# One head and batch per partition for q, k and v, with kv on four row groups

## The chip, the cores and the metric

The kernel runs on one core of a Trainium2 chip. Its time is the device time of one execution in microseconds (us). Five engines work side by side: TensorE (PE, with its weight loads as PEld), VectorE (DVE), ScalarE (ACT), GpSimd (POOL) and SyncE (SP). Each takes its instructions in order and waits on semaphores for the others. Sixteen DMA engines move data between HBM and the on-chip memory (SBUF); here POOL, SP and ACT issue the transfers. PE writes its sums to PSUM.

## The reference

All data is float32. A linear attention is followed by a mixing of the sequence's 64 lowest frequencies.

```python
# q, k, v: (8, 8, 576, 64); w_phi: (64, 128)
def phi(x):
    proj = np.einsum('bhsd,df->bhsf', x, w_phi)
    proj = proj - np.max(np.abs(proj), axis=-1, keepdims=True)
    return np.concatenate([np.exp(proj), np.exp(-proj)], axis=-1)
q_p, k_p = phi(q), phi(k)
kv = np.einsum('bhsf,bhsd->bhfd', k_p, v)
z = np.sum(k_p, axis=2)
num = np.einsum('bhsf,bhfd->bhsd', q_p, kv)
den = np.einsum('bhsf,bhf->bhs', q_p, z)[..., None] + 1e-06
# x: num / den as (8, 576, 512); w_r, w_i: (64, 512, 512); w_ch: (512, 512)
X = np.fft.rfft(x, axis=1); Xr, Xi = X.real[:, :64], X.imag[:, :64]
Yr = einsum('bmd,mde->bme', Xr, w_r) - einsum('bmd,mde->bme', Xi, w_i)
Yi = einsum('bmd,mde->bme', Xr, w_i) + einsum('bmd,mde->bme', Xi, w_r)
u = x + irfft(Yr + 1j * Yi, n=576)      # the other frequencies are 0
out = u + maximum(u @ w_ch, 0)
```

The two weight arrays hold 134 MB, q, k and v together 28 MB, the output 9.4 MB.

## The kernel before

**Units.** The attention is cut into 16 units: a group g of two heads (four of them) by a pair bp of two batches (four). A unit has 4 x 576 = 2304 rows of 64 values of each of q, k and v. They lie in SBUF as 128 partitions x 18 rows. A partition belongs to a head (64 partitions each) and holds nine neighbouring rows of the first batch and nine of the second: `(h p) b (c d)`, with c = 9 in `load` (L94). Chunk n of 18 is column n of this layout. `load_k` and `load_q` convert to bf16 on the way; `load_v` (L121) keeps float32. POOL issues them, but SP the first two units' v; the last unit's v is issued by SP in three parts of 57, 64 and 7 partitions (`load_v_parts`, L113).

**A unit's steps.** `turn_k` and `turn_q` (L125) transpose two columns at a time on PE and ACT copies the result to kT and qT, which hold features on partitions. `rows` (L153) multiplies by w_phi (`w2blk` holds it twice, for two columns) with rows on partitions, and DVE takes the largest absolute value per row: mk for k, m for q. `exp_k` (L173) exponentiates k's product with both signs on ACT (AB). k's largest values go into v instead: `weigh_v` makes ee, `weigh_v2` multiplies v by it into va, and a 65th column makes z. `kv` (L201) contracts AB with va over the rows, 64 partitions of one head at a time, into two `one` buffers; ACT copies the sums to kvz (`keep_kv`). For q, `shift_q` (L223) turns m and makes mT, `cols_q` (L239) makes the product with features on partitions and subtracts the largest value by a second product, and `exp_q` (L260) exponentiates it with both signs (AQ). `num` (L276) contracts AQ with kvz, and DVE divides into xs. `freq` (L305) takes x to frequencies with the table CF, and `keep_x` keeps them in XT.

**The order.** Every engine's instructions stay in the order in which the program gives them (`InOrder`, L27; each of these instructions has L37 in the profile). The loop from L534 handles, in one pass, the steps of four neighbouring units: P (frequencies), Q (kv and num), K (rows and exponentials) and R (transposes). The part of a pass that the prediction speaks of, in order: `Q.exp_q(0)`, `K.rows_k(0)`, `K.exp_k(0)`, `Q.weigh_v2()` and the load of a later v, `P.freq()`, `P.keep_x()`, `Q.cols_q(1)`, `Q.exp_q(1)`, `K.rows_k(1)`, `K.exp_k(1)`, `Q.kv()`, `K.rows_q(0)`, `K.rows_k(2)`, `K.rows_q(2)`, `K.rows_q(1)`, `Q.cols_q(2)`, `Q.keep_kv()`, `Q.exp_q(2)`, `K.exp_k(2)`, `K.weigh_v()`, `R.turn_k`, `K.shift_q()`, `Q.num(0)`, `K.cols_q(0)`, `R.turn_q`, `Q.num(12)`.

**Buffers.** PSUM is given out by two helpers: `one` (L69), four buffers of one bank, and `two` (L72), two buffers of two banks, each taken in turn; a new use waits for the last reader of the buffer's old content. Inputs have two buffers each (`pin`).

**Weights.** 64 loads of w_r and w_i (tile wt: one real or imaginary array, eight modes, 128 of 512 channels; 2.1 MB read, stored as bf16) go through nine slots and a few borrowed places. `next_w` (L374) issues a load on POOL and `mix` (L480) uses it; `some` (L519) puts mixes into the passes. After the loop the rest of the weights are mixed (L1031 on), while `fill` runs the work of the output: `Channels` (x times w_ch), `Absorb` and the inverse tables. When the last weights have come, `finish` and `Pair` (L869) make the last sums and store the output by SP, two row chunks at a time; `back` (L767) picks the inverse table's column for a chunk.

Of the kernel before, what the change touches and what calls it, by code (L numbers as in the profile page):

```python
# [10 lines left out]
F32 = mybir.dt.float32  # L11
BF16 = mybir.dt.bfloat16
# [31 lines left out]
def kernel(  # L44
# [49 lines left out]
    def load(t, src, g, bp, eng):  # L94
        eng.dma_start(
            t.rearrange("p b c d -> p b (c d)"),
            src[2 * bp:2 * bp + 2, 2 * g:2 * g + 2].rearrange("b h (p c) d -> (h p) b (c d)", c=9),
        )


    class Unit:
# [3 lines left out]
        def load_k(self):  # L105
            self.kb = pin.tile([128, 2, 9, D_], BF16, name="kb")
            load(self.kb, k, self.g, self.bp, pool)

        def load_q(self):
            self.qb = pin.tile([128, 2, 9, D_], BF16, name="qb")  # L110
            load(self.qb, q, self.g, self.bp, pool)

        def load_v_parts(self):  # L113
            self.vn = pin.tile([128, 2, 9, D_], F32, name="vn")
            dst = self.vn.rearrange("p b c d -> p b (c d)")
            src = v[2 * self.bp:2 * self.bp + 2, 2 * self.g:2 * self.g + 2].rearrange(
                "b h (p c) d -> (h p) b (c d)", c=9)
            for p0, p1 in ((0, 57), (57, 121), (121, 128)):
                sp.dma_start(dst[p0:p1], src[p0:p1])

        def load_v(self, eng=pool):  # L121
            self.vn = pin.tile([128, 2, 9, D_], F32, name="vn")
            load(self.vn, v, self.g, self.bp, eng)

        def turn(self, src, dst, flat, part):  # L125

            rows = src.rearrange("p i c d -> p (i c d)")
            lo, hi = ((0, 4), (4, 9))[part]
            ptr = one([128, hi - lo, 128], BF16)
            for j in range(lo, hi):  # L130
                if flat or j < 4:
                    pe.transpose(ptr[:, j - lo, :], rows[:, j * 128:(j + 1) * 128], ident_b)
                elif j < 8:
                    n = 9 + 2 * (j - 4)
                    pe.transpose(ptr[:, j - lo, :], rows[:, n * 64:n * 64 + 128], ident_b)
                else:
                    for i in range(2):
                        pe.transpose(ptr[64 * i:64 * i + 64, j - lo, :], src[:, i, 8, :], ident_b)
            act.copy(dst[:, lo:hi, :], ptr)

# [49 lines left out]
        def weigh_v2(self):  # L190
            ee = self.ee
            self.va = pm.tile([128, 2, 18, 65], BF16, name="va", bufs=1)
            dve.tensor_copy(self.va[:, :, :, 64], ee)
            for ab in range(2):
                dve.tensor_tensor(
                    out=self.va[:, ab, :, 0:64], in0=self.vn.rearrange("p i c d -> p (i c) d"),
                    in1=ee[:, ab, :].unsqueeze(2).to_broadcast([128, 18, 64]), op=ALU.mult,
                )
            self.kvz = pm.tile([128, 2, 2, 2, 65], BF16, name="kvz", bufs=1)

        def kv(self):  # L201
            pk = [one([128, 2, 2, 65]) for h in range(2)]
            for i in range(2):
                for ab in range(2):
                    for c in range(9):
                        n = 9 * i + c
                        for h in range(2):
                            r = slice(64 * h, 64 * h + 64)
                            pe.matmul(
                                pk[h][:, i, ab, :], lhsT=self.AB[n // 8][r, ab, n % 8, :],  # L210
                                rhs=self.va[r, ab, n, :],
                                start=(i == ab == c == 0), stop=(i == ab == 1 and c == 8),
                            )
            self.pk2 = pk

        def keep_kv(self):
            for h in range(2):
                act.copy(self.kvz[:, h], self.pk2[h])

# [40 lines left out]
        def exp_q(self, i):  # L260
            if i == 0:
                self.AQ = []
            if i < 2:
                t = pm.tile([128, 2, 2, 2, 2, 64, 2], BF16, name="AQ", bufs=3)
            else:
                t = pm.tile([128, 2, 2, 128], BF16, name="AQr", bufs=1)
            for ab in range(2):
                if i < 2:
                    o = t[:, ab].rearrange("f c j h p a -> f a c (j h) p")
                    src = self.pa.rearrange("f c (a j) (h p) -> f a c (j h) p", a=2, h=2)  # L270
                else:
                    o, src = t[:, ab], self.pa
                act.activation(o, src, ACT.Exp, scale=1.0 - 2.0 * ab)
            self.AQ.append(t)

        def num(self, n0):  # L276

            pn = one([128, 6, 65])
            for n in range(n0, n0 + 6):
                h = n % 2  # L280
                if n < 16:
                    i, c = n // 8, n % 8 // 2
                    for ab in range(2):
                        pe.matmul(
                            pn[:, n - n0, :],
                            lhsT=self.AQ[i][:, ab, c % 2, c // 2, h].rearrange("f p a -> f (p a)"),
                            rhs=self.kvz[:, h, i, ab, :], start=(ab == 0), stop=(ab == 1),
                        )
                else:
                    for i in range(2):  # L290
                        r = slice(64 * i, 64 * i + 64)
                        for ab in range(2):
                            pe.matmul(
                                pn[r, n - n0, :],
                                lhsT=self.AQ[2][:, ab, i, 64 * h:64 * h + 64],
                                rhs=self.kvz[:, h, i, ab, :], start=(ab == 0), stop=(ab == 1),
                            )
# [7 lines left out]
        def freq(self):  # L305
            g, bp = self.g, self.bp
            px = one([128, 4, 2, 2, 32])
            for i in range(2):
                for out, d, t in ((px[:, 0:4:3, :, i], 0, slice(0, 2)),
                                  (px[:, 2, :, i], 1, 0), (px[:, 1, :, i], -1, 1)):  # L310
                    for c in range(5):
                        n = 8 * i + 2 * c if c < 4 else 16
                        at = 16 + ((g * NP + bp) * 18 + n) * D_ + d
# [78 lines left out]
    for p0 in (0, 64):  # L392
        pool.iota(si[p0:p0 + 64, 4:5], [[1, 1]], base=8, channel_multiplier=9)
    pi = const.tile([128, 1], I32, name="pi")
    pool.iota(pi, [[0, 1]], base=0, channel_multiplier=1)
    nine = const.tile([128, 64], F32, name="nine")
    pool.iota(nine.bitcast(I32), [[9, 64]], base=0, channel_multiplier=0)
    mi = scr[:, 2048:2112].bitcast(I32)
# [20 lines left out]
    dve.tensor_copy(odd[:, 0:1], odd[:, 2:3].bitcast(I32))  # L419
    dve.tensor_scalar_mul(out=odd[:, 1:2], in0=odd[:, 0:1], scalar1=-0.5)  # L420
    dve.tensor_scalar(out=sf[:, 0:4], in0=sf[:, 0:4], scalar1=0.5, scalar2=odd[:, 1:2],
# [112 lines left out]
    for n in range(-2, len(units) + 1):  # L534
# [55 lines left out]
        elif R and n + 4 == len(units):  # L590
            kept = pin.tile([128, 2, 9, D_], BF16, name="kb").rearrange(
                "p b c d -> p (b c d)")[:, 0:1024].rearrange("p (f m) -> p f m", m=8)
            assert not any(key[0] == 1 for key in mixq)
# [83 lines left out]
    def inverse_tables():  # L677
# [6 lines left out]
        for c in range(4):  # L684
            for a in range(2):
                dve.tensor_scalar_add(
                    out=tok[:, 128 * c:128 * c + 128].rearrange("k (p a) -> k a p", a=2)[:, a],
                    in0=nine, scalar1=float(4 * a + c))
        for i in range(2):
            dve.tensor_scalar_add(out=tok[:, 512 + 64 * i:576 + 64 * i], in0=nine, scalar1=8.0)  # L690
        used = [0, 0]
# [52 lines left out]
    class Channels:  # L744
# [15 lines left out]
        def product(self):  # L760
# [4 lines left out]
            act.copy(xw[:, self.bp, self.n, :], pf)  # L765

    def back(p, c, bp, table, src, r, start):  # L767

        if c < 8:
            pe.matmul(p, lhsT=table[r, c % 4, :], rhs=src[r, 2 * bp + c // 4, :],  # L770
                      start=start, stop=True)
# [97 lines left out]
    class Pair:  # L869
# [32 lines left out]
        def sums(self, side, a):  # L902
            (bp, n), at, z = self.items[a], self.at(side, a), self.z(side)
            start = not self.based(side)
            if self.straight:
                pe.matmul(at, lhsT=CM[n // 4][:, n % 4], rhs=ends[z], start=start,
                          stop=True)
# [28 lines left out]
        def store(self):  # L936
# [3 lines left out]
            for p in parts:  # L940
                a = slice(p[0], p[-1] + 1)
                self.add(a)
                if self.n8:
                    sp.dma_start(
                        bass.AP(tensor=out.tensor, offset=out.offset + (2 * bp * S_ + 8) * DMODEL,
                                ap=[[9 * DMODEL, 128], [2 * S_ * DMODEL, 2], [1, DMODEL]]),
                        self.o)
                else:
                    rows = out[2 * bp + n // 4]
                    sp.dma_start(  # L950
                        bass.AP(tensor=rows.tensor,
                                offset=rows.offset + (n % 4 + p[0]) * DMODEL,
                                ap=[[9 * DMODEL, 64], [4 * DMODEL, 2], [1, len(p) * DMODEL]]),
                        self.o[:, a].rearrange("p a e -> p (a e)"))
# [197 lines left out]
```

## Time and profile before

| what | us |
|---|---|
| three runs, median (lowest to highest) | 431.27 (430.65 to 433.17) |
| the profiled execution | 430.94 |
| its span, first to last instruction | 428.7 |
| PE busy, PEld busy | 321.2, 195.5 |
| DVE busy | 303.6 |
| ACT busy | 300.6 |
| POOL busy | 127.8 |
| end of the loop over units | 284 |
| last weights landed | 393 to 396 |

The mean granted TensorE clock was 0.94. Busy times add up over stages that differ: the loop over units, the rest of the weights with the output's work, and the tail. PE's busy time counts pipelined products. The page gives groups of instructions as `engine op out<-in, shape xcount | busy, mean ns | idle before`; a timeline line begins with the start and length in us and ends with the idle time before it and what ended it.

### The profile page before, as it was taken

The page shows a single profiled execution, that of the slowest core. Times are in us where ns is not written, and L with a number is a line of the kernel's source. Part 1 is how long each engine was busy: PE and PEld are TensorE (multiplying, and loading weights), DVE is VectorE, ACT ScalarE, POOL GpSimd, SP SyncE. Part 2 cuts the span into 40 slices and gives each one's busy share as a digit, 9 for nine tenths or more (in the row PEclk, how much of TensorE's full clock was granted, in tenths as well). Part 3 has the DMA queues.
Part 4 walks back from the last instruction along what each step waited for, and adds up shares of the span by engine and source line. Part 5 has one row for each costly group of instructions (what it writes and reads, how often), then busy time and mean ns, then how long its engine had stood idle before and what let it go on. Part 6 is the DMA issues. An engine that isn't in the chain of part 4 may idle for free.

```text
span 428.7 us, 10215 instructions
## 1 busy us (share of the span) xinstructions
PE 321.2 (75%) x4243; PEld 195.5 (46%) x4291; DVE 303.6 (71%) x592; ACT 300.6 (70%) x490; POOL 127.8 (30%) x167
## 2 busy tenths in 40 slices
PE   1666676678696677786795767867899789878994
PEld 1345555456364445554564545543454333333321
DVE  6668668766776776877877858868645546964695
ACT  3788788896887996977978848766644335553883
POOL 6232132123121213213122321220122037691661
PEclk9989799989999998998989969898999989999998
DMA  9999999999999999999999999999999999999798
GB/s 215 209 211 211 237 214 238 219 231 238 240 210 230 220 238 238 238 210 240 210 240 218 232 240 233 212 211 213 212 212 212 212 212 212 212 212 194 190 398 344
DMA packets 50040, 97.71 MB, mean 228 GB/s; under 512 B 2379, under 2 KB 11723, under 8 KB 49995
## 3 DMA queue, kind: packets, MB, share of 16 engines
q0 software_dynamic: 45152, 85.27, 101.6%
q1 hardware_dynamic: 4682, 11.73, 7.6%
q8 instruction: 33, 0.54, 0.5%
q10 hardware_dynamic: 160, 0.07, 0.1%
q14 instruction: 13, 0.10, 0.1%
HBM read 163.64 MB, written 9.44 MB: 404 GB/s over the span
## 4 chain that ended last, share of the span: by engine, by line
DMA 34%; PE 24%; ACT 22%; DVE 14%; issue 4%; POOL 1%; ACTq 0%; POOLq 0%; DVEq 0%
DMA wt<-in_moe_w_i_dram 28%; ACT AQ L37 9%; PE one L37 8%; PE pt L37 8%; DMA kb<-in_k_dram 6%; ACT AB L37 6%; DVE m L37 6%; PE two L37 5%; PE pp L37 3%; ACT qT L37 2%; ACT XT L37 2%; DVE xw L37 2%; DVE mk L37 1%; DVE mT L37 1%; DVE xs L37 1%
## 5 line engine op out<-in xcount | busy, mean ns | idle before, releaser
L37 ACT ACTIVATE AQ<-two 128x1024 bf16<-128x1024 f32 x64 | 80.5, 1347 | 2.2 <-PE two L37 2.1
L37 ACT ACTIVATE AB<-two 128x1024 bf16<-128x1024 f32 x64 | 62.7, 1051 | 4.5 <-DVE mk L37 4.2
L37 DVE TENSOR_REDUCE m<-two 128x8 f32<-128x1024 f32 x32 | 39.1, 1223 | 19.9 <-PE two L37 19.6
L37 POOL DMA_DIRECT2D wt<-in_moe_w_i_dram x30 | 22.2, 739 | 85.3 <-PE one L37 44.1
L37 DVE TENSOR_REDUCE mk<-two 128x8 f32<-128x1024 f32 x32 | 38.9, 1219 | 9.4 <-PE two L37 9.4
L37 ACT CAST xw<-pt 128x512 bf16<-128x512 f32 x39 | 22.9, 586 | 31.8 <-PE pt L37 31.6
L37 DVE TENSOR_TENSOR va<-vn,ee 128x1152 bf16<-128x1152 f32 x32 | 42.8, 1383 | 1.8 <-DMA vn<-in_v_dram 1.8
L37 PE MATMUL pt<-wchb,xT 128*128 128x512 bf16 x135 | 37.8, 394 | 7.2 <-DVE xT L37 2.4
L37 PE MATMUL two<-w2blk,qT 128*128 128x256 bf16 x128 | 21.9, 299 | 24.0 <-ACT AQ L37 12.3
L37 POOL DMA_DIRECT2D wt<-in_moe_w_r_dram x32 | 23.6, 739 | 52.6 <-PE one L37 25.9
L37 PEld LDWEIGHTS <-xs 128*128 128x128 bf16 x624 | 31.2, 102 | 13.3 <-issue 6.8
L37 ACT COPY qT<-one 128x512 bf16<-128x512 bf16 (+1 forms) x32 | 19.0, 642 | 20.8 <-PE one L37 20.7
L37 PEld LDWEIGHTS <-qT 128*128 128x128 bf16 x144 | 14.5, 103 | 38.2 <-issue 34.9
L37 PEld LDWEIGHTS <-XT 128*32 128x32 bf16 x584 | 16.8, 148 | 29.8 <-issue 16.9
L37 POOL DMA_DIRECT2D kb<-in_k_dram x16 | 11.4, 713 | 62.1 <-PE one L37 47.8
L37 PE MATMUL two<-mT,minus 96*128 96x512 bf16 x64 | 26.2, 410 | 2.9 <-issue 0.7
L37 DVE TENSOR_TENSOR xs<-one,rd 128x384 bf16<-128x384 f32 x48 | 26.8, 557 | 1.6
L37 PE MATMUL one<-wt,XT 128*32 128x512 bf16 x272 | 23.9, 439 | 3.4 <-ACT XT L37 3.4
L37 DVE TENSOR_TENSOR xs<-pa,xs 128x512 bf16<-128x512 f32 x27 | 17.7, 685 | 12.1 <-PE pa L37 10.3
L37 PE MATMUL one<-kvz,AQ 128*128 128x65 bf16 x512 | 25.3, 200 | 1.1 <-ACT qT L37 0.8
L37 PEld LDWEIGHTS <-AQ 128*128 128x128 bf16 x512 | 22.6, 103 | 7.0 <-issue 3.0
L37 POOL TENSOR_TENSOR xw<-rl,xw 128x512 bf16<-128x512 f32 x20 | 22.7, 1169 | 7.9 <-ACT rl L37 7.6
(161 smaller groups left out, 733.5 us busy)
## 6 DMA issues: line engine op xcount, KB each, us to landing
wt<-in_moe_w_r_dram POOLq DMA_DIRECT2D x29, 1024.0 KB, 27.7
wt<-in_moe_w_i_dram POOLq DMA_DIRECT2D x27, 1024.0 KB, 28.0
out_dram<-of SPq DMA_DIRECT2D x15, 512.0 KB, 3.6
vn<-in_v_dram POOLq DMA_DIRECT2D x13, 576.0 KB, 25.1
kb<-in_k_dram POOLq DMA_DIRECT2D x16, 288.0 KB, 21.4
qb<-in_q_dram POOLq DMA_DIRECT2D x16, 288.0 KB, 19.7
xs<-in_moe_w_i_dram POOLq DMA_DIRECT2D x2, 1024.0 KB, 23.9
out_dram<-of SPq DMA_DIRECT2D x6, 256.0 KB, 4.1
```

Of the source, the lines that this page charges most:

```text
L37: ins = f(*args, **kwargs)
```

## The change

A partition now holds 18 neighbouring rows of one head and one batch. For q and k the partition is (head, 32, batch) and a load is one transfer; v's partition is (batch, head, 32) and a load is two transfers of 64 partitions, one a batch. ACT's copies of the transposed q and k sort the batches apart, so that AB's partitions match va's. kv works on four groups of 32 partitions; its sums lie in one `two` buffer and two `one` buffers, and keep_kv takes three copies instead of two. The last v comes in four parts. AQ is written as one run with its input read across four columns. The row numbers behind the tables for the frequencies and the output's rows follow the new layout. The loop, the order of the steps and the weights' loads stay.

```diff
     def load(t, src, g, bp, eng):
         eng.dma_start(
-            t.rearrange("p b c d -> p b (c d)"),
-            src[2 * bp:2 * bp + 2, 2 * g:2 * g + 2].rearrange("b h (p c) d -> (h p) b (c d)", c=9),
+            t.rearrange("p c d -> p (c d)"),
+            src[2 * bp:2 * bp + 2, 2 * g:2 * g + 2].rearrange("b h (p c) d -> (h p) b (c d)", c=18),
         )
...
         def load_v_parts(self):
...
-            for p0, p1 in ((0, 57), (57, 121), (121, 128)):
-                sp.dma_start(dst[p0:p1], src[p0:p1])
+                "b h (p c) d -> b (h p) (c d)", c=18)
+            for p0, p1 in ((0, 57), (57, 64), (64, 121), (121, 128)):
+                sp.dma_start(dst[p0:p1], src[p0 // 64, p0 % 64:(p1 - 1) % 64 + 1])
 
         def load_v(self, eng=pool):
-            self.vn = pin.tile([128, 2, 9, D_], F32, name="vn")
-            load(self.vn, v, self.g, self.bp, eng)
+            self.vn = pin.tile([128, 18, D_], F32, name="vn")
+            dst = self.vn.rearrange("p c d -> p (c d)")
+            src = v[2 * self.bp:2 * self.bp + 2, 2 * self.g:2 * self.g + 2].rearrange(
+                "b h (p c) d -> b (h p) (c d)", c=18)
+            for b in range(2):
+                eng.dma_start(dst[64 * b:64 * b + 64], src[b])
...
             for j in range(lo, hi):
-                if flat or j < 4:
...
+                m = j if flat or j > 7 else 2 * (j % 4) + j // 4
+                pe.transpose(ptr[:, j - lo, :], rows[:, m * 128:(m + 1) * 128], ident_b)
+            act.copy(dst[:, lo:hi, :].rearrange("p j (b q) -> p j b q", b=2),
+                     ptr.rearrange("p j (q b) -> p j b q", b=2))
...
         def kv(self):
-            pk = [one([128, 2, 2, 65]) for h in range(2)]
-            for i in range(2):
+            low = two([128, 2, DMODEL])[:, :, 0:130].rearrange("p h (a d) -> p h a d", a=2)
+            high = [one([128, 2, 65]) for h in range(2)]
+            out = [low[:, 0], low[:, 1]] + high
+            for i in range(3):
                 for ab in range(2):
-                    for c in range(9):
-                        n = 9 * i + c
-                        for h in range(2):
-                            r = slice(64 * h, 64 * h + 64)
+                    for n in range(8 * i, min(8 * i + 8, 18)):
+                        for p in range(4):
+                            r = slice(32 * p, 32 * p + 32)
                             pe.matmul(
-                                pk[h][:, i, ab, :], lhsT=self.AB[n // 8][r, ab, n % 8, :],
+                                out[p][:, ab, :], lhsT=self.AB[i][r, ab, n % 8, :],
                                 rhs=self.va[r, ab, n, :],
...
         def keep_kv(self):
+            low, high = self.pk2
+            act.copy(self.kvz[:, :, 0], low)
             for h in range(2):
-                act.copy(self.kvz[:, h], self.pk2[h])
+                act.copy(self.kvz[:, h, 1], high[h])
...
             if i < 2:
-                t = pm.tile([128, 2, 2, 2, 2, 64, 2], BF16, name="AQ", bufs=3)
+                t = pm.tile([128, 2, 2, 2, 2, 32, 4], BF16, name="AQ", bufs=3)
...
                 if i < 2:
-                    o = t[:, ab].rearrange("f c j h p a -> f a c (j h) p")
-                    src = self.pa.rearrange("f c (a j) (h p) -> f a c (j h) p", a=2, h=2)
+                    o = t[:, ab].rearrange("f c b h p a -> f c (b h p) a")
+                    src = self.pa.rearrange("f c a s -> f c s a")
...
-    dve.tensor_scalar_mul(out=odd[:, 1:2], in0=odd[:, 0:1], scalar1=-0.5)
+    dve.tensor_scalar_mul(out=odd[:, 1:2], in0=odd[:, 0:1], scalar1=-8.0)
+    dve.tensor_tensor(out=sf[:, 4:5], in0=sf[:, 4:5], in1=odd[:, 1:2], op=ALU.add)
+    dve.tensor_scalar(out=odd[:, 2:3].bitcast(I32), in0=pi, scalar1=0, scalar2=3,
+                      op0=ALU.logical_shift_right, op1=ALU.bitwise_and)
+    dve.tensor_copy(odd[:, 1:2], odd[:, 2:3].bitcast(I32))
+    dve.tensor_scalar_mul(out=odd[:, 1:2], in0=odd[:, 1:2], scalar1=-0.5)
...
-        for i in range(2):
-            dve.tensor_scalar_add(out=tok[:, 512 + 64 * i:576 + 64 * i], in0=nine, scalar1=8.0)
+        for a in range(2):
+            for i in range(2):
+                at = 512 + 64 * i
+                dve.tensor_scalar_add(
+                    out=tok[:, at:at + 64].rearrange("k (p a) -> k a p", a=2)[:, a],
+                    in0=nine.rearrange("k (p a) -> k a p", a=2)[:, 0], scalar1=float(16 + a))
...
                 if self.n8:
+                    for i, (bp, n) in enumerate(self.items):
+                        sp.dma_start(
...
+                                    ap=[[18 * DMODEL, 64], [DMODEL, 2], [1, DMODEL]]),
+                            self.o[:, i])
+                else:
+                    b, j = place(n)
+                    rows = out[2 * bp + b]
                     sp.dma_start(
...
+                        bass.AP(tensor=rows.tensor, offset=rows.offset + (j + p[0]) * DMODEL,
+                                ap=[[18 * DMODEL, 32], [4 * DMODEL, 4], [1, len(p) * DMODEL]]),
```

## The prediction

> **What bounds the kernel now.** I read the page first, its slices and the line on HBM, to see which resource is never idle.
>
> ```profile
> span 428.7 us, 10215 instructions
> ...
> DMA  9999999999999999999999999999999999999798
> ...
> HBM read 163.64 MB, written 9.44 MB: 404 GB/s over the span
> ```
>
> The DMA engines are full in every slice until the last three. Reads are over at about 393 us (next view): 163.64 MB / 393 us = 416 GB/s. Then the chain of waits, in order of time, for what ends last.
>
> ```profile
> 328.49 37.24 DMA wt<-in_moe_w_i_dram
> 366.01 27.12 DMA wt<-in_moe_w_i_dram
> 393.18 0.67 PE pt L37 x12
> ```
>
> A weight load issued at 328.49 lands at 365.73, one issued at 366.01 at 393.13. By the timeline of POOL, four whole loads (2.10 MB read each) and four of 0.79 MB land between those two: 11.5 MB in 27.4 us, 421 GB/s. So the stream is a queue about 27 us deep that runs at one rate in bytes, and its last landing starts a tail of 35.6 us. Third, the waits of PE from 330 to 395 us (us in total, times, longest), to see how far compute is behind that stream.
>
> ```profile
> PE pt L37 <- DMA wt<-in_moe_w_i_dram: 3.1, 2, 1.6
> ...
> PE pt L37 <- DMA wt<-in_moe_w_r_dram: 1.5, 2, 1.2
> ```
>
> PE waits for weights 4.6 us in all, and from 284 to 330 us not once. Landings set beside the products that read them say the same: the products come 3 to 9 us after the landing until 330 us, 0.5 to 6 until 377, and within 0.1 us from 380 us on. Two bounds lie close together: the stream, and compute with some 4.5 us to spare. Fourth, the loop over units, which ends at 284 us: PE, then ACT, around one kv.
>
> ```profile
> 60.33 0.60 PE L37 MATMUL two<-w2blk,kT 128*128 128x256 bf16 x4 [0.75 <-ACT AB L37]
> 60.86 0.98 PE L37 MATMUL one<-va,AB 64*128 64x65 bf16 x50
> ...
> 63.42 0.60 PE L37 MATMUL two<-w2blk,qT 128*128 128x256 bf16 x4 [1.24 <-ACT AQ L37]
> ```
>
> ```profile
> 60.82 2.55 ACT L37 ACTIVATE AQ<-two 128x1024 bf16<-128x1024 f32 x2
> 63.14 2.02 ACT L37 ACTIVATE AB<-two 128x1024 bf16<-128x1024 f32 x2
> 64.93 0.77 ACT L37 CAST kvz<-one 128x260 bf16<-128x260 f32 x2
> ```
>
> kv's 72 products run from 60.86 to about 62.2, hidden under AQ. rows_q(0) starts at 63.42, the moment AQ ends, since it takes over the `two` buffer that AQ read. From there the chain goes on through two reductions (m), the shift (mT), cols_q(0), the copies qT, and AQ of the next unit: AQ ends again at 78.5, a period of 15.1 us.
>
> **The change, part by part.** Durations are of the profiled execution: 430.94 us, of which 428.7 are span; the runs have a median of 431.27, so one stands for the other.
>
> *The new wait.* kv's sums now lie in one `two` buffer and two `one` buffers. `two` has two buffers taken in turn; the order was rows_k(0), cols_q(1), rows_k(1), rows_q(0), rows_q(1), cols_q(0), and kv comes in fourth. So kv takes the buffer of cols_q(1) and waits for AQ (63.4); rows_q(0), which had that buffer, now takes that of rows_k(1) and waits for AB, two exponentials of 1.05 later: 65.5. rows_q(1) takes kv's buffer and waits for the copy kvz after it. kv itself is 144 products of 32 rows in place of 72 of 64. Now one takes 1.34 us / 72 = 19 ns with two row groups; four groups side by side give 10 ns (1.4 us), no gain from the smaller groups 19 ns (2.7 us). The first hides under AB. So rows_q(0) is late by 2.1 to 2.8 us; I take 2.4, between them. The trace has no product of 32 contracted rows beside three others. Queued behind kv on PE are rows_q, rows_k(2), cols_q(2) and the transposes of the next k, and DVE's reductions wait for those. In seven units PE already waits for kvz after kv (8.5 us in all); there 1.2 us of the delay is there today, and 0.65 to 1.4 is left; I take 1.0. Of the 15 passes with both kv and rows_q: 8 x 2.4 + 7 x 1.0 = 26.2 us (ends 21.4 and 32.2).
>
> [...]
>
> *q's exponentials.* AQ and AB do the same arithmetic on 1024 elements; AQ writes every other bf16, AB a run.
>
> ```profile
> L37 ACT ACTIVATE AQ<-two 128x1024 bf16<-128x1024 f32 x64 | 80.5, 1347 | 2.2 <-PE two L37 2.1
> L37 ACT ACTIVATE AB<-two 128x1024 bf16<-128x1024 f32 x64 | 62.7, 1051 | 4.5 <-DVE mk L37 4.2
> ```
>
> The new AQ writes runs but reads elements 512 B apart. Nothing in this trace reads so. Bounds: 1051 (as AB) and 1347 (the penalty only moves to the other side). I take 1051, because its writes are then AB's; 4 x 0.296 = 1.18 us a pass, all on the chain, 17.7 us over 15.
>
> *Copies and setup.* qT's and kT's copies read every other element: free, or slower in AQ's ratio (1.28), 0.33 us a pass for qT's 1.18 us on the chain, 5 in all; kT's are covered by mT and cols_q. I take 1. One transpose fewer a unit saves 0.06 us off the path. Four more small DVE operations of 0.15 to 0.25 us stand ahead of ident_b, for which PE waits 8.7 us at the start: 0.7 late. Two more operations of 0.28 us in the inverse tables, on the chain at 286: 0.5.
>
> *Compute in sum:* 26.2 - 17.7 + 1 + 0.7 + 0.5 = 10.7 us, less 4.5 to spare: +6.2. Ends: 21.4 + 1.2 - 17.7 - 4.5 = +0.4 and 32.2 + 6.2 - 17.7 - 4.5 = +16.2.
>
> *The stream.* k and q: 32 loads, each 256 packets of 1152 B written becoming 128 of 2304. By the packets' own lengths two of 107 ns become one of about 173 x 4608/4096 = 195: 19 ns x 4096 / 16 engines = 4.9 us, over the 1.12 by which packets overlap 4.3. By landings a k or q load comes 1.42 us after the one before it, and its bytes at a weight's rate (4.95 us for 2.10 MB) are 1.39: 32 x 0.03 = 1.0 us. The queue delivers by landings: -1.0. v has packets of 4608 B already (1.46 us a load) and its bytes stay; two halves at today's rate cost nothing. The last v, on SP: the 57-row part runs on three engines (its packets come by threes), 38 packets each of 2304 B. Two 57-row parts are 38 each of 4608 B: 38 x 88 ns = 3.3 us more on these, less 0.7 for the 64-row part. They ran 3 to 4 us ahead of the slowest, and now use that up; then all weights land that much later: +2 (ends 0 and +2.6). 2,300 more instructions add 7 fetch packets to 33 of 0.95 us: +0.5. Sum of the stream: +1.5; -3.8 to +3.1 at the ends. POOL issues 13 more loads of 0.7 us and its window of eight outstanding holds fewer bytes, but the queue stays over 15 us deep. SP's two more stores in the tail lie between others.
>
> *Together:* the later of the two decides: 430.9 + 6.2 = 437.1, said as 437.
>
> **Rivals.** *The halves of v run at half rate.* Each half writes 64 neighbouring partitions. If these can take only half of what 128 take, each half needs as long as a whole load now: 13 x 1.46 = 19 us more in the stream, which has no spare, 430.9 + 19 + 1.5 = 451; if the engines' skew (landings of one load's 16 engines spread over 0.8 us at the start, 5.3 at the end) takes half of it away, 442. For: v alone arrives as f32, all that is read is written. Against: no half-width f32 load from POOL is in the trace.
>
> [...]
>
> *AQ gains nothing* (its read is as dear as its write was): 6.2 + 17.7 = 24 us, 455; partly, 447.
>
> *The stream hides it all, and the time is not slower.* Place: the end of the loop at 284 us. If the loop's delay stays below 4.5 us, 0.3 a pass (kv hides wholly under AB, and the seven late passes lose nothing), only the stream counts: -3.8 to +3.1, so 427 to 434, with 431 the likeliest. For: DMA is full throughout. Against: the chain by which rows_q(0) is late is long and has no slack in its 15.1 us.
>
> **How the numbers follow.** The forecast (434 to 442, likeliest 437) 0.42; v at half rate (441 to 452) 0.27; AQ without gain (447 to 460) 0.10; hidden 0.21. A measurement of this kernel tells 0.5% from nothing, 2.2 us; of the hidden case a quarter lies below 429.1 and three quarters within 2.2 us: faster 0.05, same 0.16, slower 0.79. The range leaves out the hidden case's faster part and the top of the dear ones: 430.5 to 452.
>
> **What would show it.** Each kv starts when AQ ends, not before; rows_q(0) starts with the end of AB, 2.1 to 2.8 us after AQ; kv takes 1.4 to 2.7 us; AQ 1051 ns; the loop ends near 294 us and PE no longer waits for weights after 376; the last weight lands near 395. If v halves land 1.4 us apart rather than 0.73, the rival holds; if PE waits for weights as before while the loop ends later, the stream hid it. I am wrong if AQ takes longer than 1347 ns or the loop keeps its 15.1 us.

## The result, and the profile after the change

The changed kernel takes 471.15 us (median of 4 runs, 469.17 to 473.56); the kernel before takes 431.3 us on the same chip. The ratio is 1.092, with a 95% interval of 1.085 to 1.099. 437 us had been predicted, with 430.5 to 452 as the range: slower was right, but the loss is 40 us and not 6. The profiled execution took 472.35 us, of which 470.6 are span.

First the page of the changed kernel: its slices, its queues, and the engines' shares of the chain of waits.

```profile
span 470.6 us, 12567 instructions
...
PEclk9656695759978879879598886957899998999998
DMA  8999999999999999999999999999999995984698
...
q8 instruction: 42, 0.69, 0.6%
...
HBM read 163.64 MB, written 9.44 MB: 368 GB/s over the span
## 4 chain that ended last, share of the span: by engine, by line
PE 43%; DVE 22%; ACT 22%; issue 9%; DMA 2%; POOL 0%; ACTq 0%; DVEq 0%; POOLq 0%
```

The same bytes are read, at 368 GB/s where it was 404, and the DMA row has holes in its last seven slices. DMA is 2% of the chain (34% before), and 9% is "issue", time for which the profile shows no wait at all (4% before). The instruction queue q8, which brings instructions, carried 42 packets (33 before). The kernel before, with its group of the reduction m, which is read further below:

```profile
q8 instruction: 33, 0.54, 0.5%
...
DMA 34%; PE 24%; ACT 22%; DVE 14%; issue 4%; POOL 1%; ACTq 0%; POOLq 0%; DVEq 0%
...
L37 DVE TENSOR_REDUCE m<-two 128x8 f32<-128x1024 f32 x32 | 39.1, 1223 | 19.9 <-PE two L37 19.6
```

So the stream no longer sets the end; compute does. The last weight lands at 430.4 us (395.8 before), and PE waits for no weight after 330 us. PEclk stands at 5 to 7 in 14 of the first 30 slices.

Next, the groups of that page that the change touches (busy us, mean ns of one, then the idle time before them and what ended it).

```profile
L37 DVE TENSOR_REDUCE m<-two 128x8 f32<-128x1024 f32 x32 | 39.1, 1221 | 66.9 <-PE two L37 66.9
L37 ACT ACTIVATE AB<-two 128x1024 bf16<-128x1024 f32 x64 | 62.2, 1030 | 18.3 <-PE one L37 13.6
L37 ACT ACTIVATE AQ<-two 128x1024 bf16<-128x1024 f32 x64 | 62.8, 1051 | 3.1 <-PE two L37 2.9
...
L37 PEld LDWEIGHTS <-AB 32*128 32x128 bf16 x2048 | 23.9, 107 | 27.8 <-issue 27.8
```

AQ takes 1051 ns, to the nanosecond what had been taken for it. Two other numbers are new: DVE's reduction m idles 66.9 us (19.9 before), and AB idles 13.6 us for PE's product `one`, which is kv (0.2 before). The 27.8 us for which kv's weight loads idle for "issue" (5.9 before) can't be read so: they are 27.6 in e17_shifted below, where kv never stands still. One pass shows both new numbers, by the timeline of ACT and PE (start, us, what, and in brackets the idle time before it).

```profile
110.13 2.00 ACT L37 ACTIVATE AQ<-two 128x1024 bf16<-128x1024 f32 x2
...
112.19 0.20 PE L37 MATMUL two<-va,AB 32*128 32x65 bf16 x2 [0.63 <-ACT AQ L37]
...
113.00 1.94 ACT L37 ACTIVATE AB<-two 128x1024 bf16<-128x1024 f32 x2 [0.86 <-PE one L37]
...
114.98 0.60 PE L37 MATMUL two<-w2blk,qT 128*128 128x256 bf16 x4 [0.40 <-ACT AB L37]
```

kv starts when AQ ends (112.14), as predicted. AB does not start there, but 0.86 us later, and rows_q(0), which had started 0.05 us after AQ, now starts after both exponentials of AB: 2.84 us after AQ. Another pass shows a loss of its own, by the timeline of PE.

```profile
52.18 0.24 PE L37 MATMUL one<-va,ABr 32*128 32x65 bf16 x1
56.85 0.21 PE L37 MATMUL one<-va,ABr 32*128 32x65 bf16 x1 [4.44 <-issue]
56.99 1.03 PE L37 MATMUL two<-w2blk,qT 128*128 128x256 bf16 x4
```

143 of kv's 144 products are done by 52.2; then PE stands still for 4.44 us with nothing to wait for, before the last one. Such standstills lie inside kv in 7 of 16 passes, 1.7 to 4.7 us each from the start of one product to the start of the next. The four products of rows_q(0) take 1.03 us here and 0.60 in the pass above: the granted clock is 0.5 here and 1.0 there.

### The profile page after: what moved, and what is told of

Its sections match the earlier page's. It is cut to its first block, busy times and chain, and to the rows that moved or that the text cites. A ratio compares the mean times of both kernels' runs of the same rounds, so it can differ in the third digit from the quotient of the medians.

```text
span 470.6 us, 12567 instructions
## 1 busy us (share of the span) xinstructions
PE 343.6 (73%) x5379; PEld 212.8 (45%) x5427; DVE 301.8 (64%) x598; ACT 288.0 (61%) x506; POOL 127.3 (27%) x180
## 4 chain that ended last, share of the span: by engine, by line
PE 43%; DVE 22%; ACT 22%; issue 9%; DMA 2%; POOL 0%; ACTq 0%; DVEq 0%; POOLq 0%
PE pt L37 15%; PE two L37 12%; PE one L37 11%; DVE m L37 10%; ACT AQ L37 9%; ACT AB L37 7%; DVE mk L37 3%; PE pa L37 3%; PE pp L37 3%; ACT XT L37 3%; DVE xs L37 2%; ACT qT L37 2%; DMA qb<-in_q_dram 2%; DVE xw L37 1%; ACT xw L37 1%
## 5 line engine op out<-in xcount | busy, mean ns | idle before, releaser
L37 DVE TENSOR_REDUCE m<-two 128x8 f32<-128x1024 f32 x32 | 39.1, 1221 | 66.9 <-PE two L37 66.9
L37 ACT ACTIVATE AB<-two 128x1024 bf16<-128x1024 f32 x64 | 62.2, 1030 | 18.3 <-PE one L37 13.6
L37 ACT ACTIVATE AQ<-two 128x1024 bf16<-128x1024 f32 x64 | 62.8, 1051 | 3.1 <-PE two L37 2.9
L37 PE MATMUL two<-va,AB 32*128 32x65 bf16 x1024 | 24.7, 211 | 24.0 <-ACT AQ L37 23.8
L37 PE MATMUL two<-w2blk,qT 128*128 128x256 bf16 x128 | 30.4, 383 | 15.6 <-ACT AB L37 14.4
L37 PEld LDWEIGHTS <-AB 32*128 32x128 bf16 x2048 | 23.9, 107 | 27.8 <-issue 27.8
L37 PE MATMUL two<-mT,minus 96*128 96x512 bf16 x64 | 28.8, 450 | 3.4 <-issue 1.5
L37 PEld LDWEIGHTS <-qT 128*128 128x128 bf16 x144 | 18.2, 130 | 28.3 <-issue 21.2
L37 PEld LDWEIGHTS <-AQ 128*128 128x128 bf16 x512 | 26.5, 113 | 8.1 <-issue 6.2
L37 PE MATMUL one<-kvz,AQ 128*128 128x65 bf16 x512 | 28.7, 214 | 1.2 <-ACT qT L37 1.2
L37 ACT ACTIVATE AQr<-one 128x256 bf16<-128x256 f32 x32 | 10.6, 383 | 30.6 <-PE one L37 30.6
L37 POOL DMA_DIRECT2D vn<-in_v_dram x26 | 13.8, 536 | 53.3 <-DVE va L37 38.5
```

Of the source, the lines that this page charges most:

```text
L37: ins = f(*args, **kwargs)
```

## The experiments

Two theories were put against each other: the new wait is the loss, only larger than predicted; or the standstills are, and come from kv's 288 PE instructions (144 products, each with its weight load; 144 before). Twelve more kernels were run; the table has them with the kernel before and the changed one, and with the time from AQ's end to the start of rows_q(0) added up over the 15 passes that have both (from the times of the timelines; left out where kv or its loads stand elsewhere):

| kernel | median us | ratio to before, 95% | AQ's end to rows_q(0), sum us |
|---|---|---|---|
| before | 431.3 | | 4.8 |
| e2_wait | 474.24 | 1.100 (1.097 to 1.102) | 47.2 |
| e3_runs | 431.75 | 1.0005 (0.999 to 1.002) | 6.6 |
| e4_halves | 443.27 | 1.027 (1.023 to 1.030) | |
| e6_twice | 441.65 | 1.022 (1.019 to 1.026) | 20.2 |
| e10_wait_runs | 459.03 | 1.064 (1.061 to 1.066) | 46.8 |
| e13_wait_runs_halves | 459.01 | 1.065 (1.060 to 1.071) | 46.6 |
| e14_wait_runs_twice | 469.02 | 1.086 (1.078 to 1.094) | 61.1 |
| after | 471.15 | 1.092 (1.085 to 1.099) | 55.7 |
| e17_shifted | 463.66 | 1.074 (1.069 to 1.079) | 45.9 |
| e16_more_AB | 466.88 | 1.082 (1.079 to 1.085) | 51.3 |
| e9_half_kv | 448.49 | 1.042 (1.037 to 1.046) | 41.3 |
| e7_two_by_two | 447.60 | 1.039 (1.034 to 1.044) | |
| e11_two_queues | 451.32 | 1.046 (1.040 to 1.051) | |

### The wait alone (e2_wait)

```diff
-            pk = [one([128, 2, 2, 65]) for h in range(2)]
+            ps = two([128, 2, DMODEL])[:, :, 0:260]
+            pk = [ps[:, h].rearrange("p (b a d) -> p b a d", b=2, a=2) for h in range(2)]
```

> The kernel before with kv's sums moved into a `two` buffer, everything else as it was (72 products of 64 rows, AQ with its gaps). Theory (the new wait is most of the loss, and is larger than predicted because AB(1) must first wait until kv has read the buffer it overwrites): kv starts when AQ ends, AB(1) starts 0.6 to 1.2 us after that, rows_q(0) starts 2.7 to 3.2 us after AQ; 15 passes of 2.7 less the 8 us that PE waits there today for kvz, less the 4.5 us to spare: 455 to 462 us. The predicted size of the wait (2.4 us in 8 passes, 1.0 in 7, less 4.5) gives 452. Rival (the wait is cheap, the standstills inside kv are the loss): at most 440 us.

474.24 us: the wait alone costs more than the whole change, 43 us. A pass of it, by the timeline of ACT and PE:

```profile
209.97 0.98 PE L37 MATMUL two<-va,AB 64*128 64x65 bf16 x50 [2.47 <-ACT AQ L37]
...
210.78 1.94 ACT L37 ACTIVATE AB<-two 128x1024 bf16<-128x1024 f32 x2 [0.85 <-PE two L37]
...
212.77 1.01 PE L37 MATMUL two<-w2blk,qT 128*128 128x256 bf16 x4 [1.47 <-ACT AB L37]
```

AB waits 0.85 us for kv although it has nothing to do with kv's sums: `AB` has three buffers, a unit uses two of them, so AB(1) of the next unit overwrites the AB[0] that kv is reading. That was harmless as long as kv ran under AQ. With it the delay is 2.84 us where kv has the full granted clock and 3.24 where it has half (0.50 to 0.54 in 9 of the 15 passes, 2 before); it is 3.15 on average and there in all 15 passes. The sum grows by 42.4 us, the time by 42.9. No standstill lies inside kv here.

The time is above the range expected, which had 8 us coming back from PE's waits for kvz. These waits are indeed gone (8.5 us before, none here), yet the loop grows by the whole sum and more: its last product of the frequencies ends at 330.9 us, and at 284.1 before. From the first kv to there PE is busy for 220.5 us here and 188.9 before, at a mean granted clock of 0.77 and 0.92. So slower products may have taken what the waits gave back; this was not tried alone.

### More buffers for AB (e16_more_AB)

```diff
-                t = pm.tile([128, 2, 8, 128], BF16, name="AB", bufs=3)
+                t = pm.tile([128, 2, 8, 128], BF16, name="AB", bufs=4)
...
-                t = pm.tile([128, 2, 2, 2, 2, 32, 4], BF16, name="AQ", bufs=3)
+                t = pm.tile([128, 2, 2, 2, 2, 32, 4], BF16, name="AQ", bufs=2)
```

> The changed kernel with four AB buffers instead of three (and two AQ buffers instead of three, for their room), so that AB(1) no longer takes over a buffer that kv is still reading. Theory (AB(1)'s wait for kv is the part of the new wait that the prediction left out): AB(1) starts within 0.1 us of AQ's end, rows_q(0) 2.0 to 2.2 us after AQ in passes without a standstill, 0.7 to 1.2 us sooner in some 9 of 15 passes: 458 to 465 us. Rival (kv holds rows_q(0) up as long by itself): 469 to 473 us.

466.88 us, 4.3 less than the changed kernel; 6 to 13 had been expected. From the groups of this kernel:

```profile
L37 ACT ACTIVATE AB<-two 128x1024 bf16<-128x1024 f32 x64 | 62.2, 1031 | 9.5 <-DVE mk L37 8.3
```

The wait for PE is gone from AB, so its cause was the buffer. But rows_q(0) stands behind kv on PE all the same: 2.1 us after AQ at full clock, 2.3 to 2.7 in most others, and 3.7 or more in passes with a standstill, as before. In several passes AB now waits for DVE's mk (8.3 us in all, 4.2 in the changed kernel), so it does not start within 0.1 us of AQ's end everywhere, as had been expected. The sum falls by 4.4 us, and the time by as much. The AQ buffer given up for it shows no cost: AQ idles 3.4 us, against 3.1.

### q's exponentials alone, and with the wait (e3_runs, e10_wait_runs)

```diff
-                    o = t[:, ab].rearrange("f c j h p a -> f a c (j h) p")
-                    src = self.pa.rearrange("f c (a j) (h p) -> f a c (j h) p", a=2, h=2)
+                    o = t[:, ab].rearrange("f c j h p a -> f c j (h p) a")
+                    src = self.pa.rearrange("f c (a j) s -> f c j s a", a=2)
```

> The kernel before with only the order in which AQ is written and read changed: runs of 128 elements, read from PSUM with a stride. Theory: AQ takes 1051 ns instead of 1347, the loop over units ends 10 to 17 us sooner, and the time stays within 427 to 431 us since the stream of weights sets the end. Rival (compute sets the end): 414 to 420 us. Second rival (the strided read costs what the gaps cost): AQ 1300 ns or more, 431 us.

431.75 us, no change; from the page of e3_runs:

```profile
DMA  9999999999999999999999999999999999999798
...
L37 ACT ACTIVATE AQ<-two 128x1024 bf16<-128x1024 f32 x64 | 62.6, 1043 | 1.5 <-PE two L37 1.3
```

AQ saves 0.3 us each time, and the stream, full as before, sets the end. The expected shorter loop did not come, though: its 14 periods take 234.8 us against 233.6. Where AQ was waited for, PE now waits for AB (11.2 us between 45 and 262 us, 8.0 before) and for kvz (10.1 and 8.0), and between 50 and 100 us the granted clock is 0.77 (0.92 before), so that the same products take longer. Why it is lower there stays open; over the whole span the two traces have 0.93 and 0.94.

> The kernel before with kv's sums in a `two` buffer and AQ written in runs, both at once (72 products of 64 rows, v in one transfer). Theory (once the loop sets the end, AQ's 4 x 0.3 us a pass count in full): 474 less 15 to 18 us, 455 to 460 us; what the changed kernel then has above this, 11 to 16 us, is kv's 288 instructions. Rival (AQ's gain is lost again in waits behind kv): 468 us or more.

459.03 us: once the loop sets the end, AQ's gain counts, 15.2 us of the 17.7 of the sum.

### v in two transfers (e4_halves, e13_wait_runs_halves)

```diff
-            load(self.vn, v, self.g, self.bp, eng)
+            dst = self.vn.rearrange("p b c d -> p b (c d)")
+            for h in range(2):
+                eng.dma_start(
+                    dst[64 * h:64 * h + 64],
+                    v[2 * self.bp:2 * self.bp + 2, 2 * self.g + h].rearrange(
+                        "b (p c) d -> p b (c d)", c=9))
```

> The kernel before with v in two POOL transfers of 64 partitions each instead of one of 128; every row lands where it did. Theory (a transfer to 64 neighbouring partitions moves at about half the rate per byte): the halves land 1.15 to 1.3 us apart, 13 loads cost 1.0 us each more of the stream, which has no spare: 440 to 446 us. Rival (full rate): halves 0.73 us apart, 430 to 432 us.

443.27 us, 12 us more. The halves land 1.29 us apart on average (56.46 and 57.71, 106.76 and 108.19; 0.74 to 1.77 in all), and a packet of theirs takes 251 ns on average where it took 180. The chain of waits, by its longest link, shows that the stream still sets the end, later:

```profile
378.01 25.55 DMA wt<-in_moe_w_i_dram
```

The last weight lands at 406.3 us, 10.5 later than before. The loop ends 13 us later too, at 297.4, so both bounds moved. The rival of the half rate was right about the transfer, for the most part: by it a half lasts as long as a whole v, 1.46 us, and 1.29 were measured (57% of a whole v's rate per byte).

> e10_wait_runs (459 us) with v in two POOL transfers of 64 partitions, as in e4_halves. Theory (the halves take about 1 us more of the DMA engines each, but the stream has some 15 us to spare once the loop is late): 457 to 461 us. Rival (the 12 us that the changed kernel has above e10_wait_runs are the halves of v): 468 to 473 us.

459.01 us against 459.03: once the loop is late, the same halves cost nothing. So they are no part of the 12 us that the changed kernel has above e10_wait_runs.

### 288 instructions (e6_twice, e14_wait_runs_twice, e9_half_kv)

```diff
+                            for t in range(2):
                                 pe.matmul(
                                     pk[h][:, i, ab, :], lhsT=self.AB[n // 8][r, ab, n % 8, :],
                                     rhs=self.va[r, ab, n, :],
-                                    start=(i == ab == c == 0), stop=(i == ab == 1 and c == 8),
+                                    start=(i == ab == c == t == 0),
+                                    stop=(i == ab == t == 1 and c == 8),
                                 )
```

> The kernel before with every product of kv issued twice: 288 PE instructions in kv as in the changed kernel, but no new wait and no new buffer. (kv and its sums are both doubled, so the quotient stays.) Theory (PE runs out of instructions when 288 come within 1.2 to 2.7 us, since they are fetched 256 at a time by a transfer that waits in the full DMA queues): standstills of 2 to 5 us with the releaser issue inside kv in 4 to 8 of 16 passes, each ending 1.2 to 1.7 us after a fetch packet has landed, 40 to 42 fetch packets; part of it hidden under AQ: 435 to 446 us. Rival (the standstills come from the order of kv's four row groups or from its PSUM buffers): no standstill over 1 us in kv, kv within 2.8 us, 430 to 433 us.

441.65 us; from the groups of e6_twice:

```profile
L37 PE MATMUL one<-va,AB 64*128 64x65 bf16 x2048 | 40.6, 196 | 7.0 <-issue 7.0
...
L37 PEld LDWEIGHTS <-AB 64*128 64x128 bf16 x2048 | 37.1, 98 | 11.2 <-issue 11.2
```

No new wait, no new buffer, other groups of rows, and the standstills are there: six over 1.2 us, the longest 3.35, 42 fetch packets as in the changed kernel. They belong to the number of instructions.

> e10_wait_runs (459 us) with every product of kv issued twice: 288 PE instructions in kv, two groups of rows at work instead of four, so kv itself is 1.1 us longer than in the changed kernel, of which AB(1) waits for half. Theory (instructions): standstills of 2 to 5 us with the releaser issue inside kv in about 7 of 16 passes, all at the same place within blocks of 256 instructions, each ending 1.3 to 1.7 us after a fetch packet's landing; 468 to 480 us. Rival (the halves of v make the 12 us): 459 to 466 us.

469.02 us, 10 above e10_wait_runs. Only three standstills exceed 1.2 us, not seven, and part of the 10 us is that AB and rows_q(0) wait for a kv that is itself longer. So this run shows that 288 instructions cost about what the changed kernel lacks, and not how the cost splits.

```diff
-                    for n in range(8 * i, min(8 * i + 8, 18)):
+                    for n in range(8 * i, min(8 * i + 8, 18), 2):
```

> The changed kernel with every second of kv's 18 columns of rows left out of the sums: 72 products of 32 rows, 144 instructions, the same buffers and the same wait. Theory (PE runs out of instructions because kv's 288 come faster than a block of 256 is fetched): no standstill over 1 us inside kv, 33 or 34 fetch packets, kv 0.6 to 1.0 us, rows_q(0) 2.4 to 2.8 us after AQ in every pass; 448 to 457 us. Rival (the standstills belong to the four row groups or to the PSUM banks): they stay in about 7 passes, 463 to 472 us.

448.49 us, with no standstill in kv and 33 packets, as expected. It lies below e10_wait_runs too, in part because kv here takes 0.58 us at full clock where 72 products of 64 rows take 1.14, and AB and rows_q(0) wait for it (41.3 us against 46.8).

### Where the blocks end (e17_shifted)

The fetch packets are the key to the standstills. In the changed kernel 42 packets of 16,384 bytes came for 10,806 recorded PE instructions, before 33 for 8,534: 257 and 259 to a packet. All seven standstills of the changed kernel lie a multiple of 254.2 recorded PE instructions apart (a few are not in the trace). The author's estimate from the two is a block of 256. PE goes on 1.3 to 1.7 us after a packet has landed. If blocks are counted from the first standstill (columns: start of kv; how many of kv's instructions come before a block ends; landing of the next fetch packet; when PE goes on; all in us but the second):

```
 50.25   33    55.51   56.85
 71.51   17    74.41   75.73
 92.00    2    94.14   95.58
148.71   17   150.66  152.14
223.71   33   228.07  229.76
303.71   17   305.60  307.01
319.47    5   322.06  323.45
the nine others: 48, 80, 81, 96, 160, 160, 208, 223, 224; none stands still
```

A pass stands still exactly where a block ends within the first 33 of kv's 288 instructions, so that the next block of 256 is used up inside kv, in 1.2 to 1.9 us. From the first block's end to the landing of the next packet 1.8 to 5.1 us pass; the DMA engines are full at that time (busy share 1.08 to 1.12 in each of the seven standstills), but whether they are what delays it was not tried. From this a test followed that leaves kv alone and only moves it in the program (its PSUM tile also moves the later `one` tiles on by one of the four buffers):

```diff
             R.turn_q(1)
+            if n == -2:
+                idle = one([128, 16])
+                for _ in range(58):
+                    pe.matmul(idle, lhsT=ident_b[0:32], rhs=ident_b[0:32, 0:16],
+                              start=True, stop=True)
```

> The changed kernel with 58 small products (32 rows, 16 columns, into a PSUM tile that nothing reads; 116 PE instructions with their weight loads) put in once, after the first unit's transposes, long before the first kv. Nothing else differs, so every later PE instruction stands 116 places further on. Theory (blocks of 256: in the changed kernel the seven standstills fall in just those units in which a block ends within the first 34 of kv's 288 instructions, so that the whole next block is used up inside kv; by this shift no block ends in the first 40 of any kv): no standstill over 1 us in any kv, perhaps one short one; 457 to 463 us, although the kernel does more. Rival (standstills come at certain times, from the load of the DMA queues, or from kv's own pattern): about seven of them again, 469 to 474 us.

463.66 us, 7.5 less, with 58 products more. kv stands still in none of the 16 passes. The waits of PE from 40 to 300 us (us in all, times, longest), first in the changed kernel, then in e17_shifted:

```profile
PE one L37 <- issue: 13.6, 5, 4.4
```

```profile
PE one L37 <- issue: 2.6, 2, 2.1
```

The sum of the table falls from 55.7 to 45.9 us, below e10_wait_runs. The 58 products themselves make the first kv 1.65 us later. The time ends 0.7 us above the range expected, and 4.6 above e10_wait_runs. Two standstills have appeared in other places, by the timeline of PE:

```profile
186.25 0.40 PE L37 MATMUL one<-w2blk,qT 128*128 128x256 bf16 x1 [2.13 <-issue]
...
320.57 1.10 PE L37 MATMUL one<-CF,xs 128*128 128x128 bf16 x23 [2.42 <-issue]
```

They end 1.7 and 1.6 us after a fetch packet has landed (184.53 and 319.02), as those in kv do. So the shift removed the standstills from kv and brought two elsewhere, which may fill much of the 4.6 us, beside the 1.65. The third copy of kvz can fill little of it: the copies take 0.73 us a pass against 0.66, some 1 us in all. None of these was tried alone.

### The changed kernel without the wait (e7_two_by_two, e11_two_queues)

```diff
-            Q.kv()
+            Q.kv(1)
...
+        if Q:
+            Q.kv(0)
+            Q.keep_kv(0)
         if K:
             K.rows_k(1)
```

Here kv(b) makes the sums of one batch, 72 products into two `one` buffers, and keep_kv(b) copies them.

> The changed kernel with kv in two halves, one batch after the other, each of 72 products of 32 rows into two `one` buffers as before the change, the first half's sums copied before AB(1). No `two` buffer, so no new wait; 288 instructions of kv, the faster AQ and the halves of v all stay. Theory (wait 43 us, standstills 10 to 20, AQ -18, halves of v 12 if the stream sets the end): rows_q(0) starts with the end of AQ again, and the stream with v in halves sets the end: 441 to 447 us, as e4_halves; standstills of PE inside kv remain in some passes and may add up to 6. Rival (the layout with 32-row products is itself the loss): over 460 us.

447.6 us, 23.6 less than the changed kernel, so the layout can run without most of its loss. The reason given was not right: the last weight came only 4.6 us after its issue, so the queue was empty and compute set the end. From the groups of e7_two_by_two:

```profile
L37 ACT ACTIVATE AB<-two 128x1024 bf16<-128x1024 f32 x64 | 62.1, 1029 | 19.0 <-DVE mk L37 13.6 <-PE one L37 4.8
```

kv's first half stands ahead of rows_k(1) on PE, so mk is late and AB waits 13.6 us for it: one wait less, another one more. Standstills remain in three passes, up to 2.3 us.

> As e7_two_by_two, with the second half of each v on SP's queue instead of POOL's. [...] Rival (a packet to one half of the partitions is slow whatever lies beside it): 441 to 447 us, as e7_two_by_two.

451.32 us, not faster; 431 to 437 us was the author's estimate for a v that costs on two queues what it did before. Since the stream does not set the end of e7_two_by_two, the time can't tell whether it does. A packet of v's halves took 224 ns on POOL's queue and 218 on SP's, against 235 in e7_two_by_two and 180 as a whole v before: little, if anything, is won back. No version was found that beats the kernel before.

## Why the prediction was wrong, point by point

**The bound.** Right. The stream sets the end before the change: a faster AQ alone changes nothing (e3_runs), and a longer stream moves the time (e4_halves: last weight 10.5 us later, time 12). After the change compute sets it. The 4.5 us to spare were right as well: what follows the loop takes 144.7 us before the change and 140.4 after it, 4.3 less.

**The new wait.** This step failed. "So rows_q(0) is late by 2.1 to 2.8 us; I take 2.4" and 1.0 in seven passes, 26.2 us in all. Alone it costs 42.9 us (e2_wait), 3.15 us a pass in all 15. The mechanism was right, and three things were left out. kv does not hide under AB, as the prediction had it: AB(1) takes over a buffer that kv reads, so it starts 0.85 to 1.25 us after AQ; in the changed kernel that is worth 4.3 us (e16_more_AB). In 9 of the 15 passes of e2_wait kv has only half the granted clock (0.50 to 0.54), which makes 2.84 us into 3.24. And no rebate shows in the seven passes that waited for kvz before: the waits went, but the loop's products slowed down (busy 220 us for 189, e2_wait). That the one took up the other is argued, not shown.

**kv's products.** That "four groups side by side give 10 ns" was nearly right: 144 products take 1.18 us at full clock, 8.2 ns each. For 64 rows in two groups they take 16 ns each (1.14 us for 72, before). What failed is what the prediction made of these instructions. The prediction counted 2,300 more instructions as seven more packets in the stream, +0.5 us (nine came); it did not see that PE itself must wait for them. That is the second missing term: 7.5 us by e17_shifted, 9 with the start that its own products delay, of the 12.1 that the changed kernel has above e10_wait_runs. It may be more, since e17_shifted stands still in two other places; how the rest splits stays open.

**q's exponentials.** Right: 1051 ns. Its 17.7 us count as 15.2 where compute sets the end (e10_wait_runs), and as nothing where it does not.

**Copies.** Taken as 1 us, with 5 as the upper end: the copies of qT take 641 ns on average, 642 before. A read of every other element costs nothing here. The third copy of kvz was not counted; it is worth about 1 us by its length.

**The stream.** +1.5 us without the halves of v; no run shows this sum alone, since the stream sets no end after the change. The halves, a rival with chance 0.27, cost 12 us where the stream sets the end (some 10 to 19 were given), and none in the changed kernel, whose stream has time to spare. Two right prices were never to be added: only the later bound counts.

**The sum**, by the runs: 431.3 + 42.9 (wait) - 15.2 (AQ) + 0 (halves) + 12.1 (288 instructions and the rest) = 471.1. The forecast had 430.9 + 26.2 - 17.7 - 4.5 + 2.2 for the rest. The loop ended at 330 us and not near 294. The wait was too small by 21 us (42.9 and the 4.5 to spare, less 26.2), and the 12 us of the instructions were missing; together they put the time above the top of the range.

## What to carry to other kernels

When an operation moves to a later place, list every buffer it reads, not only those it writes: whoever overwrites them next waits too, here AB. Price a wait on the critical chain in every pass, and at the clock that the traces show after such a wait (here 0.50 to 0.54 in 9 of 15 passes of e2_wait), before subtracting what other waits might give back. And count PE instructions by the stretch: many small products in a burst can be faster than the instructions arrive (kv's 288 in 1.2 to 1.9 us were, in 7 of 16 passes), and whether they are depends on where they stand in the program (in none of the 16 in e17_shifted).

## What the runs showed of the hardware

- Instructions came in packets of 16,384 bytes, one for 257 recorded PE instructions (10,806 and 42 packets in the changed kernel; 256 is an estimate from this and the 254.2 between standstills). A burst of 288 in 1.2 to 1.9 us stood still for 1.7 to 4.7 us when, by that count, it held a whole packet, while the DMA engines were full (1.08 to 1.12); 116 instructions put in far ahead of it removed all seven from kv, and two appeared elsewhere (e17_shifted).
- Four row groups of 32 at work together took a product every 8.2 ns at full clock, two groups of 64 one every 16 ns (1.14 us for 72).
- A faster ACT did not shorten the loop: in e3_runs PE waited for other things, and the granted clock between 50 and 100 us was 0.77 against 0.92, one trace of each. Whether the faster ACT is the cause of the lower clock was not shown.
- ACT read PSUM elements 512 B (changed kernel) or 1024 B apart (e3_runs) and wrote runs at 1051 and 1043 ns for 1024 elements, as fast as AB from a run (1051); 1347 ns was the price of the gaps on the writing side.
